# Polysketch attention feeding a gated feed-forward layer: one cast moved to GpSimd, two weight loads moved ahead of a key load, larger dummy products, and a planner's durations rewritten

## The chip, the cores and the metric

The kernel runs on one core of a Trainium2 chip. A core has five engines that run on their own and meet at semaphores: TensorE (PE, with its weight loads shown as PEld), VectorE (DVE), ScalarE (ACT), GpSimd (POOL) and SyncE (SP), which here only issues DMAs. The metric is the device time of one execution in microseconds (us). The profile gives one execution's span, which is a little shorter than its device time.

## The reference

```python
# batch 4, heads 4, seq 1088, head_dim 32, r = 8; x: 4352 tokens x 128; d_ff 1536
def phi(x):                                     # 64 features from 32
    a = np.einsum('rd,bhsd->bhsr', S1, x)
    b = np.einsum('rd,bhsd->bhsr', S2, x)
    return np.einsum('bhsi,bhsj->bhsij', a, b).reshape(*x.shape[:-1], r * r)
q_p, k_p = phi(q), phi(k)
kv  = np.einsum('bhsf,bhsd->bhfd', k_p, v)
num = np.einsum('bhsf,bhfd->bhsd', q_p, kv)
den = np.einsum('bhsf,bhf->bhs', q_p, np.sum(k_p, axis=2))[..., None] + 1e-06
x   = (num / den).transpose(0, 2, 1, 3).reshape(4352, 128)
out = np.maximum(x @ w_gate, 0) * (x @ w_val) @ w_out
```

Inputs and output are float32. The feed-forward part is done with float16 operands, most of the sketches in float32.

## The kernel before, in words

The work has two parts that run through each other. For each of the four batches, attention makes a 128 x 128 block matrix `bz` from keys and values, and then the columns of `xT`, the feed-forward input, from queries. The feed-forward part takes `xT` in groups of two or four blocks of 128 tokens, and each group in units of at most 512 columns.

Keys (class `K`): load `k`, transpose on DVE (L525, `kT`), sketch on PE (`ksk`, L536), transpose back (L549, `kab`), multiply the two sketches out to 64 features (`kphi`, L593, `kp`; POOL for most, DVE for two pieces of batch 0, which first need a copy in PSUM, L557), and sum `kp` times `v` on PE (`kv`, L606). `v` must first be cast to float16 in two halves (`vc`, L599). L613 copies the result to `bz`.

Queries (classes `Q` and `G`): transposes (L1024), sketches (L728), a division by the denominator, then the product to 64 features (`qphi`, L859, `qqp`). The features are transposed (`qpt`), for the first three groups on PE (`qtr`, L877, copied by ACT on L884) and for the other seven by a DMA that SP issues (L867). `num` (L893) multiplies by `bz`, and ACT (L905), or DVE for the first group (L900), writes `xT`. For the first group alone the reciprocals go through ACT (L777), PE (L782) and ACT (L787).

Feed-forward (class `F`), per unit: `g` (L950) and `v` (L962) on PE, relu on ACT (L955), the product `h` on DVE (L972) or, in every sixth unit, a copy on ACT (L967) and the product on POOL (L977), then `o` (L984) on PE. At the end of a group ACT copies the sum (L992) and SP stores it (L1001, L1006).

The weights come as float32, in thirds: `wg0..2`, `wv0..2` (columns) and `wo0..2`. Each third lands in a buffer that later holds the keys, queries or values of batches 1 to 3 (`wst`), and is cast to float16 from there (L425 on ACT, L427 on POOL, by the table `CAST`). So the loads of `v1`, `k2`, `v2`, `k3`, `q3` and `v3` have to wait for casts. All loads, stores and transposing DMAs go through SP's one queue, in program order.

The order of the instructions is not written out by hand. A planner inside the kernel (`Plan`) knows a duration for every step, a landing time for every early load (`LAND`), and a due time for every unit (`T0 + u * U`, plus `D1` from unit 6 on), and lists the steps of each engine in the order in which its own reckoning would start them. Each engine then runs its list strictly in order. The durations change nothing on the chip but this order, and the number of dummy products.

Dummies: `warm(n)` fills the gaps that the planner sees on PE before the first feed-forward unit with products of a zero tile, `n` columns in all, written to a PSUM bank that nothing reads (L330). Their number is fixed when the program is built.

Of the kernel before, what the change touches and what calls it, by code (L numbers as in the profile page):

```python
# [146 lines left out]
def kernel(  # L147
# [115 lines left out]
    load_w(0)  # L263
    load_w(1)
    load_wo(0)
    load_k(nc.sync, 1)
    load_w(2)
    load_wo(1)
    load_wo(2)
    nc.sync.dma_start(out=q_sb[1], in_=flat(q, 1))  # L270
# [55 lines left out]
    def warm(n):  # L326

        while n >= 32:
            m = min(n // 32 * 32, 128)
            nc.tensor.matmul(PS[:, W_BANK, 0:m], zero, zero[:, 0:m], start=True, stop=True)  # L330
            n -= m

    warm(3584)
    S_BANK = 6
# [46 lines left out]
    P.banks[W_BANK] = 13.0  # L381
    P.banks[S_BANK] = 6.0
    l_sx = Lease()
    T0, U, SLACK = 11.0, 0.68, 0.25
    D1 = 0.2

    TURN = ["ACT"] * 3 + ["DMA"] * 7

# [7 lines left out]
        return cols / 960.0 + 0.085  # L396

    def act(cols):
        return cols / 1200.0 + 0.045

    def pool(cols):
        return cols * 0.00188 + 0.07

    LAND = {"k0a": 3.6, "S": 4.3, "k0b": 4.25, "q0a": 5.6, "q0b": 7.35, "v0": 9.95,
            "wg0": 10.35, "wv0": 11.0, "wg1": 11.65, "wv1": 12.3, "wo0": 12.95, "k1": 15.6,
            "wg2": 16.25, "wv2": 16.9, "wo1": 17.5, "wo2": 18.1, "q1": 19.5}
    land = {n: P.landed(n, t) for n, t in LAND.items()}
    P.free["DMA"] = LAND["q1"]

    def bank(l, i=0):  # L410
# [4 lines left out]
    sa_op = P.add("DVE", "SA", 0.22, make_SA, [land["S"]], rec=0.07)  # L415
    wb_op = P.add("DVE", "WB", 0.15, make_WB, [land["S"]], rec=0.07)

    CAST = {"wg0": "ACT", "wv0": "POOL", "wg1": "ACT", "wv1": "POOL", "wo0": "POOL",
            "wg2": "ACT", "wv2": "ACT", "wo1": "ACT", "wo2": "POOL"}
    wcast = {}  # L420

    def cast(w, i, eng):
# [9 lines left out]
                         rec={"ACT": 0.13, "DVE": 0.07, "POOL": 0.0}[e])  # L432


    def load(name, fn, after):
        n = 4 if name[0] == "v" else 1
        i = P.add("SP", f"{name} issue", 0.44 * n, fn, after, rec=1.95 - 0.44 * n)
# [6 lines left out]
    load("k3", lambda: load_k(nc.sync, 3), [wcast["wg0"], wcast["wv0"], land["q2"]])  # L444
    load("q3", lambda: load_q(nc.sync, 3), [wcast["wg1"], wcast["wv1"], land["q2"]])
    load("v3", lambda: load_vs(3), [land["v2"]])

    class K:


        def __init__(self, b, prev):
# [13 lines left out]
                                               [(0, NC // 2), (NC // 2, NC)])]  # L465
            for n, l in enumerate(self.las):
                self.sks.append(P.add(
                    "PE", f"ksk {b} {n}", sk32(KX * 32) + 0.04 if b else (0.62, 0.68)[n],
                    lambda n=n: self.sk(n), t1 + [ws_op], take=[l]))
            if prev is None and b == 0:  # L470
                sx = P.add("PE", "sx", 0.25, make_sx, self.sks, take=[l_sx])
# [13 lines left out]
            self.wc_op = P.add("DVE", f"wc {b}", 0.11, self.wc, [w], drop=[lw], rec=0.07)  # L485
            phis = []
            cut = [(0, 2), (2, 4), (4, 6), (6, KX)] if b else [(0, 2), (2, 4), (4, 6), (6, 8), (8, KX)]
            own = [3, 4] if b == 0 else []
            lb = Lease()
            self.lb = lb  # L490
            for n, (lo, hi) in enumerate(cut):
# [11 lines left out]
                else:  # L503
                    phis.append(P.add("POOL", f"kphi {b} {lo}", pool(cols),
                                      lambda lo=lo, hi=hi: self.phi(nc.gpsimd, lo, hi), dep))
            vc = [P.add("ACT", f"vc {b} {h}", 0.58, lambda h=h: self.vc(h), [land[f"v{b}"]],
                        rec=0.13) for h in range(2)]
            lm = Lease()
            self.lm = lm
            self.kvs = []  # L510
# [87 lines left out]
        def vc(self, h):  # L598
            nc.scalar.copy(out=v16[self.b][:, 2 * h:2 * h + 2], in_=v32[self.b][:, 2 * h:2 * h + 2])  # L599

        def kv(self, lo, hi, pp):
            m = bank(self.lm)
# [28 lines left out]
    class Q:  # L631
# [3 lines left out]
        def __init__(self, b, x0, n, i, ks, qt1, old):  # L635
            self.b, self.x0, self.n, self.ks = b, x0, n, ks
            i = i % NS
            self.abc, self.an = q_abc[i], q_an[i]
            self.dn, self.rd, self.bw = q_dn[i], q_rd[i], bw[i]
            first = b == 0 and x0 == 0  # L640
            self.first = first
            name = f"{b},{x0}"
            cols = n * 32
            wcs = [kk.wc_op for kk in ks]
            if first:
                la, lc = Lease(), Lease()
# [8 lines left out]
                at = P.add("PE", f"qaT {name}", 0.85, self.aT, qt1 + [sa_op], take=[lt])  # L655
                ate = P.add("ACT", f"qaTe {name}", act(256), self.aTe, [at], drop=[lt], rec=0.13)
                s2 = [P.add("PE", f"qc {name}", 0.45, self.cx, [ate, ks[0].zc_op], take=[lc])]
                o1 = P.add("DVE", f"bw {name}", dve(cols) + 0.03, self.mul_ps, s2 + [t2] + old,
                           drop=[lc], rec=0.09)
                e, eng = "DVE", nc.vector  # L660

            else:
                self.l4 = [Lease(2), Lease(2)]
                s1 = P.add("PE", f"qsk {name}", cols / 600.0 + 0.28 + 0.37 * (n > NX),
                           self.sk, qt1 + wcs + [wq_op], take=self.l4)
# [25 lines left out]
            self.t2_op = t2  # L691
            self.last = []
# [106 lines left out]
    class G:  # L799


        def __init__(self, qs, b, ks, x0, n, i, col, old, how):
# [6 lines left out]
            if qs.first:  # L809
                for x in range(n):  # L810
                    phis.append(P.add("DVE", f"qphi {name} {x}", 0.31,
                                      lambda x=x: self.phi(nc.vector, x, x + 1), [qs.o4],
                                      drop=[qs.la], rec=0.07))
                qs.la.left -= n
            else:
                phis.append(P.add("POOL", f"qphi {name}", pool(n * 256),
                                  lambda: self.phi(nc.gpsimd, 0, n), [qs.o4] + old))
            if how == "DMA":
                pt = P.add("SP", f"qtd {name}", 1.28, self.xpose, phis + old, rec=0.7)
                pt = P.add("DMA", f"qtd {name}", 0.6, None, [pt], rec=0.5)  # L820
            else:
                lt = Lease()
# [84 lines left out]
    class F:  # L907


        def __init__(self, u, grp, qg, js, prev, old):  # L910
# [14 lines left out]
            vv = P.add("PE", f"v {u}", cost, self.v, [qg.x_op, wcast[f"wv{third}"]], take=[lv], due=t + 0.2)  # L925
            if self.pool:
                a2 = P.add("ACT", f"vcp {u}", act(cols), self.vcp, [vv], drop=[lv], rec=0.13,
                           due=t + 0.6)
                h = P.add("POOL", f"hp {u}", 1.18, self.hp, [a, a2, old], due=t + 1.3)
# [113 lines left out]
    for n, (b, x0, w, parts) in enumerate(sets):  # L1043
# [6 lines left out]
        for gb, y, m in parts:  # L1050
# [80 lines left out]
```

## Time and profile before

| what | value |
| --- | --- |
| device time, median of 3 runs | 101.46 us (101.31 to 104.93) |
| device time of the profiled execution | 102.56 us |
| its span | 100.8 us |
| PE busy | 95.1 us, 94% of the span |
| DVE, ACT, POOL busy | 83.8, 82.2, 59.9 us |
| bytes moved by DMA | 13.28 MB |
| dummy products (L330) | 85, 7.7 us, all before 14 us |
| granted TensorE clock | 1.00 |

A matmul's printed time holds some 0.2 us that the next one overlaps: one of 512 columns is printed with 0.38 us, and a row of them follows at 0.22 us each. So PE's busy time hides short pauses, which show where one product starts later than the pace of the rows allows. A square bracket in the timeline gives the idle time before an instruction, and who ended it.

### The profile page before, as it was taken

To read this page: it belongs to the slowest core of one execution; us is meant where nothing else is said; L and a number is where in the kernel's file an instruction comes from. 1 tells how busy PE (TensorE), PEld (TensorE's weight loads), DVE (VectorE), ACT (ScalarE), POOL (GpSimd) and SP (SyncE) were. 2 spreads that over 40 slices of the span, in tenths; PEclk is the share of its full clock that TensorE was granted. 3 is DMA by queue.
4 is the path that set the end of the run, shared out by engine and by line. 5 is a ranking of instruction groups with operands and counts; after the bars stand their busy time and mean duration, and the time that the engine had idled before them with its cause. 6 is when DMAs were issued, how large, how long until landed. Compare 5 with 4: busy or idle time off the path is not lost.

```text
span 100.8 us, 3139 instructions
## 1 busy us (share of the span) xinstructions
PE 95.1 (94%) x1191; PEld 66.4 (66%) x1191; DVE 83.8 (83%) x181; ACT 82.2 (82%) x162; POOL 59.9 (59%) x64
## 2 busy tenths in 40 slices
PE   6999997999999899999999999999999999999960
PEld 6959895678775466656756676667666666667940
DVE  5989959899999989999998679978768587795960
ACT  3411968997999978999977769899899999989940
POOL 7157269399999399349973993489960314033100
PEclk9999999999999999999999999999999999999999
DMA  2999999499943696300426003001481300120031
GB/s 44 321 272 294 408 403 417 166 309 272 386 131 108 145 136 163 104 7 0 104 52 156 7 0 104 7 7 37 121 182 37 81 24 0 52 59 0 4 100 52
DMA packets 16783, 13.28 MB, mean 132 GB/s; under 512 B 8064, under 2 KB 14464, under 8 KB 16768
## 3 DMA queue, kind: packets, MB, share of 16 engines
q1 hardware_dynamic: 16736, 13.08, 45.8%
q8 instruction: 9, 0.15, 0.6%
q14 instruction: 6, 0.05, 0.1%
q10 hardware_dynamic: 32, 0.00, 0.0%
HBM read 9.14 MB, written 2.23 MB: 113 GB/s over the span
## 4 chain that ended last, share of the span: by engine, by line
PE 78%; POOL 7%; ACT 5%; DMA 3%; issue 2%; DVE 2%; ACTq 0%
PE ps L984 19%; PE ps L950 18%; PE ps L962 17%; PE ps L330 7%; POOL qqp L859 4%; PE ps L893 3%; ACT g_sb L955 3%; PE ps L728 3%; DMA qpt<-qqp 3%; PE ps L536 2%; PE ps L606 2%; POOL kp L593 1%; PE ps L564 1%; PE ps L877 1%; DVE qabc L734 1%
## 5 line engine op out<-in xcount | busy, mean ns | idle before, releaser
L972 DVE TENSOR_TENSOR ht<-g_sb,ps 128x512 f16<-128x512 f16 (+1 forms) x87 | 55.4, 672 | 10.1 <-ACT g_sb L955 5.5
L955 ACT ACTIVATE g_sb<-ps 128x512 f16<-128x512 f32 (+1 forms) x103 | 57.1, 610 | 4.9 <-PE ps L950 4.1
L950 PE MATMUL ps<-xT,wg 128*128 128x512 f16 (+1 forms) x120 | 38.3, 348 | 0.4 <-ACT wg L425 0.4
L984 PEld LDWEIGHTS <-ht 128*128 128x128 f16 x408 | 28.8, 98 | 14.0 <-POOL ht L977 2.5
L984 PE MATMUL ps<-wo,ht 128*128 128x128 f16 x408 | 36.5, 219 | 0.2
L962 PE MATMUL ps<-xT,wv 128*128 128x512 f16 (+1 forms) x120 | 36.5, 348 | 0.0
L977 POOL TENSOR_TENSOR ht<-g_sb,v_sb 128x512 f16<-128x512 f16 x16 | 18.7, 1170 | 19.3 <-ACT v_sb L967 13.2
L593 POOL TENSOR_TENSOR kp<-kab 128x512 f16<-128x512 f32 (+1 forms) x15 | 17.1, 1162 | 5.0 <-DVE kab L549 5.0
L962 PEld LDWEIGHTS <-wv 128*128 128x128 f16 x120 | 13.0, 115 | 5.1 <-issue 1.1
L859 POOL TENSOR_TENSOR qqp<-qan,qabc 128x1024 f16<-128x1024 f32 (+1 forms) x9 | 15.7, 1763 | 0.1
L950 PEld LDWEIGHTS <-wg 128*128 128x128 f16 x120 | 13.1, 114 | 3.7 <-issue 0.9
L967 ACT COPY v_sb<-ps 128x512 f32<-128x512 f32 x16 | 9.7, 605 | 0.0
L330 PE MATMUL ps<-zero 128*128 128x128 f16 (+2 forms) x85 | 7.7, 257 | 1.0 <-DVE maskkv L295 1.0
L330 PEld LDWEIGHTS <-zero 128*128 128x128 f16 x85 | 6.7, 119 | 1.4 <-DVE maskkv L295 1.0
L992 ACT ACTIVATE o_sb<-ps 128x512 f32<-128x512 f32 (+1 forms) x10 | 5.5, 546 | 1.9 <-PE ps L984 1.9
L599 ACT CAST v<-v 128x576 f16<-128x576 f32 x8 | 5.3, 700 | 1.5 <-DMA v<-in_v_dram 1.4
L734 DVE STREAM_TRANSPOSE qabc<-ps 128x512 f32<-128x512 f32 (+2 forms) x8 | 5.4, 695 | 0.7 <-PE ps L728 0.6
L1024 DVE STREAM_TRANSPOSE qT<-q_sb 128x576 f32<-128x576 f32 (+4 forms) x10 | 6.0, 611 | 0.0
L905 ACT CAST xT<-ps 128x512 f16<-128x512 f32 (+1 forms) x9 | 4.9, 550 | 1.1 <-PE ps L893 1.1
L893 PE MATMUL ps<-qpt,bz 128*128 128x512 f16 (+2 forms) x26 | 5.3, 305 | 0.4 <-DMA qpt<-qqp 0.4
L525 DVE STREAM_TRANSPOSE kT<-k_sb 128x544 f32<-128x544 f32 (+2 forms) x8 | 5.6, 725 | 0.0
L606 PEld LDWEIGHTS <-kp 128*128 128x128 f16 (+1 forms) x72 | 3.6, 98 | 1.3 <-issue 0.2
(85 smaller groups left out, 63.9 us busy)
## 6 DMA issues: line engine op xcount, KB each, us to landing
v<-in_v_dram SPq DMA_DIRECT2D x15, 144.0 KB, 4.5
out_dram<-o_sb SPq DMA_DIRECT2D x28, 64.0 KB, 1.7
k_sb<-in_k_dram SPq DMA_DIRECT2D x3, 544.0 KB, 5.4
q_sb<-in_q_dram SPq DMA_DIRECT2D x3, 544.0 KB, 7.1
k_sb<-in_moe_w_out_dram SPq DMA_DIRECT2D x2, 256.0 KB, 5.9
q_sb<-in_q_dram SPq DMA_DIRECT2D x1, 416.0 KB, 5.2
k_sb<-in_k_dram SPq DMA_DIRECT2D x1, 288.0 KB, 2.9
k_sb<-in_k_dram SPq DMA_DIRECT2D x1, 256.0 KB, 3.0
```

What stands on the lines that cost most here:

```text
L330: nc.tensor.matmul(PS[:, W_BANK, 0:m], zero, zero[:, 0:m], start=True, stop=True)
L593: eng.tensor_tensor(out=self.kp[:, lo:hi].rearrange("p x g (i a c) -> p (x g i) a c", i=2, a=R), in0=src[:, 0, :, :, None].to_broadcast([1 ...
L734: nc.vector.transpose(self.abc[:, 0:self.n, 2 * i:2 * i + 2].rearrange("p x h f -> p h x f"), PS[:, b0:b1 + 1, 0:self.n * 32].rearrange("p ...
L859: eng.tensor_tensor(out=self.qp[:, lo:hi].rearrange("p x g (i a c) -> p (x g i) a c", i=2, a=R), in0=a_in[:, :, :, None].to_broadcast([128 ...
L893: nc.tensor.matmul(o[:, 0:n * 128].rearrange("f (x t) -> f x t", x=n)[:, :, t], self.ks[b or 0].bz[:, p], self.pt[:, 0:n, p, t], start=(p ...
L950: nc.tensor.matmul(bank(self.lg)[:, y * W:(y + 1) * W], wblock(wg, j), x, start=True, stop=True, skip_group_check=True)
L955: nc.scalar.activation(out=self.gs[:, 0:self.cols], in_=bank(self.lg)[:, 0:self.cols], func=ACTF.Relu)
L962: nc.tensor.matmul(bank(self.lv)[:, y * W:(y + 1) * W], wblock(wv, j), x, start=True, stop=True, skip_group_check=True)
L967: nc.scalar.copy(out=self.vs, in_=bank(self.lv))
L972: nc.vector.tensor_tensor(out=self.ht[:, 0:w], in0=self.gs[:, 0:w], in1=bank(self.lv)[:, 0:w], op=ALU.mult)
L977: nc.gpsimd.tensor_tensor(out=self.ht, in0=self.gs, in1=self.vs, op=ALU.mult)
L984: nc.tensor.matmul(o[:, s], self.ht[:, y * W + s * 128:y * W + (s + 1) * 128], wo[:, j // 4, (j % 4) * DM:(j % 4 + 1) * DM], start=(j == 0 ...
```

## The change

- The second half of batch 0's `v` is cast by POOL instead of ACT. In its place POOL casts `wg2`, `wv2` and `wo1`, which ACT did, and ACT casts `wv1`, which POOL did. DVE's share of batch 0's `kphi` goes from two pieces to one; POOL does the other.
- SP issues the loads of `wg2` and `wv2` ahead of batch 1's keys.
- SP issues the loads of `k3`, `q3` and `v3` behind the transposing DMAs of batch 1 (the step `gs[4].turn`), instead of ahead of them.
- A dummy has up to 512 columns, by reading the same 128 columns of zeros up to four times, and before the first unit 0.1 us less is filled in each gap from the time `WARM` on.
- The planner's numbers (`U`, `D1`, `LAND`, `act`, and several steps) are others, so many steps stand elsewhere in their engine's list.

In the built program there are 23 dummies in place of 85, of 8,512 columns in all in place of 10,624. The other products, and the DMAs, are the same in number and size.

```diff
     load_wo(0)
+    load_w(2)
     load_k(nc.sync, 1)
-    load_w(2)
     load_wo(1)
...
         while n >= 32:
-            m = min(n // 32 * 32, 128)
-            nc.tensor.matmul(PS[:, W_BANK, 0:m], zero, zero[:, 0:m], start=True, stop=True)
-            n -= m
+            m, w = (min(n // 128, 4), 128) if n >= 128 else (1, n // 32 * 32)
+            nc.tensor.matmul(PS[:, W_BANK, 0:m * w], zero,
+                             zero[:, None, 0:w].to_broadcast([128, m, w]), start=True, stop=True)
+            n -= m * w
...
-    T0, U, SLACK = 11.0, 0.68, 0.25
-    D1 = 0.2
+    T0, U, SLACK = 11.0, 0.65, 0.25
+    D1 = 0.7
...
-        return cols / 1200.0 + 0.045
+        return cols / 1200.0 + 0.062
...
-            "wg0": 10.35, "wv0": 11.0, "wg1": 11.65, "wv1": 12.3, "wo0": 12.95, "k1": 15.6,
-            "wg2": 16.25, "wv2": 16.9, "wo1": 17.5, "wo2": 18.1, "q1": 19.5}
+            "wv0": 10.99, "wg1": 11.63, "wv1": 12.27, "wo0": 12.91, "wg2": 14.75, "wv2": 15.39,
+            "k1": 16.75, "wo1": 17.39, "wo2": 18.03, "q1": 19.39}
...
-    CAST = {"wg0": "ACT", "wv0": "POOL", "wg1": "ACT", "wv1": "POOL", "wo0": "POOL",
-            "wg2": "ACT", "wv2": "ACT", "wo1": "ACT", "wo2": "POOL"}
+    CAST = {"wg0": "ACT", "wv0": "POOL", "wg1": "ACT", "wv1": "ACT", "wo0": "POOL",
+            "wg2": "POOL", "wv2": "POOL", "wo1": "POOL", "wo2": "POOL"}
...
-            own = [3, 4] if b == 0 else []
+            own = [4] if b == 0 else []
...
-            vc = [P.add("ACT", f"vc {b} {h}", 0.58, lambda h=h: self.vc(h), [land[f"v{b}"]],
-                        rec=0.13) for h in range(2)]
+            vc = [P.add(e, f"vc {b} {h}", 0.66 if e == "POOL" else 0.58,
+                        lambda h=h, e=e: self.vc(h, e), [land[f"v{b}"]],
+                        rec=0.0 if e == "POOL" else 0.13)
+                  for h, e in enumerate(["ACT", "ACT" if b else "POOL"])]
...
+    for n in ("k3", "q3", "v3"):
+        issue[n].after.append(gs[4].turn)
+        gs[4].turn.succ.append(issue[n])
...
-                warm(int((o.start - at) * (1200 if o.start < WARM else 2280)))
+                warm(int((o.start - at) * 1200) if o.start < WARM else
+                     int((o.start - at - 0.1) * 2280))
```

More of the change, by code (lines that the diff above doesn't have):

```diff
@@ L398, in act @@
     def act(cols):
-        return cols / 1200.0 + 0.045
+        return cols / 1200.0 + 0.062
     def pool(cols):
         return cols * 0.00188 + 0.07
-    LAND = {"k0a": 3.6, "S": 4.3, "k0b": 4.25, "q0a": 5.6, "q0b": 7.35, "v0": 9.95,
-            "wg0": 10.35, "wv0": 11.0, "wg1": 11.65, "wv1": 12.3, "wo0": 12.95, "k1": 15.6,
-            "wg2": 16.25, "wv2": 16.9, "wo1": 17.5, "wo2": 18.1, "q1": 19.5}
+    LAND = {"k0a": 3.6, "S": 4.3, "k0b": 4.25, "q0a": 5.4, "q0b": 7.35, "v0": 9.95, "wg0": 10.35,
+            "wv0": 10.99, "wg1": 11.63, "wv1": 12.27, "wo0": 12.91, "wg2": 14.75, "wv2": 15.39,
+            "k1": 16.75, "wo1": 17.39, "wo2": 18.03, "q1": 19.39}
     land = {n: P.landed(n, t) for n, t in LAND.items()}
@@ L432 @@
                          rec={"ACT": 0.13, "DVE": 0.07, "POOL": 0.0}[e])
+    issue = {}
     def load(name, fn, after):
         n = 4 if name[0] == "v" else 1
-        i = P.add("SP", f"{name} issue", 0.44 * n, fn, after, rec=1.95 - 0.44 * n)
+        issue[name] = i = P.add("SP", f"{name} issue", 0.44 * n, fn, after,
+                                rec=1.95 - 0.44 * n)
         land[name] = P.add("DMA", name, 2.7 if n == 4 else 1.4, None, [i], rec=0.15)
@@ L443 @@
     load("v2", lambda: load_vs(2), [wcast["wg2"], wcast["wv2"], land["v1"]])
-    load("k3", lambda: load_k(nc.sync, 3), [wcast["wg0"], wcast["wv0"], land["q2"]])
-    load("q3", lambda: load_q(nc.sync, 3), [wcast["wg1"], wcast["wv1"], land["q2"]])
+    load("k3", lambda: load_k(nc.sync, 3), [wcast["wg0"], wcast["wv0"]])
+    load("q3", lambda: load_q(nc.sync, 3), [wcast["wg1"], wcast["wv1"]])
     load("v3", lambda: load_vs(3), [land["v2"]])
@@ L467, in __init__ @@
                 self.sks.append(P.add(
-                    "PE", f"ksk {b} {n}", sk32(KX * 32) + 0.04 if b else (0.62, 0.68)[n],
+                    "PE", f"ksk {b} {n}", sk32(KX * 32) + 0.04 if b else (0.47, 0.52)[n],
                     lambda n=n: self.sk(n), t1 + [ws_op], take=[l]))
@@ L596, in phi, with vc @@
                 in1=bs[:, :, None, :].to_broadcast([128, n, R, R]), op=ALU.mult)
-        def vc(self, h):
-            nc.scalar.copy(out=v16[self.b][:, 2 * h:2 * h + 2], in_=v32[self.b][:, 2 * h:2 * h + 2])
+        def vc(self, h, e):
+            o, i = (t[self.b][:, 2 * h:2 * h + 2] for t in (v16, v32))
+            nc.scalar.copy(out=o, in_=i) if e == "ACT" else nc.gpsimd.tensor_copy(out=o, in_=i)
         def kv(self, lo, hi, pp):
@@ L654, in __init__ @@
                 self.lt = lt
-                at = P.add("PE", f"qaT {name}", 0.85, self.aT, qt1 + [sa_op], take=[lt])
+                at = P.add("PE", f"qaT {name}", 0.62, self.aT, qt1 + [sa_op], take=[lt])
                 ate = P.add("ACT", f"qaTe {name}", act(256), self.aTe, [at], drop=[lt], rec=0.13)
@@ L663, in __init__ @@
                 self.l4 = [Lease(2), Lease(2)]
-                s1 = P.add("PE", f"qsk {name}", cols / 600.0 + 0.28 + 0.37 * (n > NX),
+                s1 = P.add("PE", f"qsk {name}", cols / 600.0 + 0.34 + 0.37 * (n > NX),
                            self.sk, qt1 + wcs + [wq_op], take=self.l4)
@@ L815, in __init__ @@
             else:
-                phis.append(P.add("POOL", f"qphi {name}", pool(n * 256),
+                phis.append(P.add("POOL", f"qphi {name}", pool(n * 256) - 0.02 * n,
                                   lambda: self.phi(nc.gpsimd, 0, n), [qs.o4] + old))
@@ L819, in __init__ @@
                 pt = P.add("SP", f"qtd {name}", 1.28, self.xpose, phis + old, rec=0.7)
+                self.turn = pt
                 pt = P.add("DMA", f"qtd {name}", 0.6, None, [pt], rec=0.5)
@@ L924, in __init__ @@
                       due=t + 0.35)
-            vv = P.add("PE", f"v {u}", cost, self.v, [qg.x_op, wcast[f"wv{third}"]], take=[lv], due=t + 0.2)
+            vv = P.add("PE", f"v {u}", cost, self.v, [qg.x_op, wcast[f"wv{third}"]], take=[lv], rec=0.07,
+                       due=t + 0.2)
             if self.pool:
@@ L928, in __init__ @@
                            due=t + 0.6)
-                h = P.add("POOL", f"hp {u}", 1.18, self.hp, [a, a2, old], due=t + 1.3)
+                h = P.add("POOL", f"hp {u}", 1.13, self.hp, [a, a2, old], rec=0.06,
+                          due=t + 1.3)
             else:
```

## The prediction

> **What bounds the kernel now.** I read the page first: its busy line, the slices, then the chain.
>
> ```profile
> span 100.8 us, 3139 instructions
> PE 95.1 (94%) x1191; PEld 66.4 (66%) x1191; DVE 83.8 (83%) x181; ACT 82.2 (82%) x162; POOL 59.9 (59%) x64
> PE   6999997999999899999999999999999999999960
> PEclk9999999999999999999999999999999999999999
> PE 78%; POOL 7%; ACT 5%; DMA 3%; issue 2%; DVE 2%; ACTq 0%
> ```
>
> PE sets the time, at a full granted clock, and its useful products are the same before and after. So only three things can move the end: when the first unit starts, where PE pauses after that, and the tail. The slices with less than 9 are at the start, at 15 to 18 us and at the end. The chain in order of time shows the first two (start, us, what):
>
> ```profile
> 12.51 0.22 PE ps L893 x2
> 12.72 1.19 PE ps L330 x22
> 13.91 0.25 PE ps L950 x2
> 14.19 1.58 ACT g_sb L955 x3
> 15.77 0.39 PE ps L877 x4
> 16.19 0.59 ACT qpt L884
> 16.77 0.50 ACT g_sb L955
> 17.27 0.52 ACT wg L425
> 17.83 0.41 PE ps L950 x2
> ...
> 28.17 3.88 POOL qqp L859 x2
> 32.05 0.28 POOL ht L977
> 32.33 2.79 DMA qpt<-qqp
> 35.17 0.60 PE ps L893 x2
> ```
>
> Here dummies (L330) stand between `num` and the first product, and later PE hands over to ACT, to POOL and to a transposing DMA. The timeline says who was late:
>
> ```profile
> 13.40 0.70 POOL L427 CAST wv<-q_sb 128x512 f16<-128x512 f32 x1 [1.82 <-DMA q_sb<-in_moe_w_val_dram]
> 14.62 2.98 POOL L859 TENSOR_TENSOR qqp<-qan,qabc 128x512 f16<-128x512 f32 x2
> 17.16 0.62 ACT L425 CAST wg<-v 128x512 f16<-128x512 f32 x1
> 25.61 4.66 SPq L216 DMA_DIRECT2D v<-in_v_dram  x4
> 30.37 1.79 SPq L1001 DMA_DIRECT2D out_dram<-o_sb  x4
> 32.33 2.68 SPq L867 DMA_TRANSPOSE qpt<-qqp  x2
> ```
>
> POOL waited 1.82 us for `wv1` to land, then cast it and `wo0`, so the second group's features (L859) started at 14.62 though their input (L794, 13.28 + 0.35) was there at 13.63. ACT cast `wg2` only at 17.16. SP was held at the loads of `v2` for 4.66 us and stored a group before it issued the transposes at 32.33; their first input was done at 28.17 + 1.96 = 30.13.
>
> PE's pauses, from start to start less the pace of the rows (256 columns 0.11 us, 128 columns 0.055): between L962 (14.86, two products) and L877 (15.75) 0.67; between L962 (16.43) and L893 (16.82) 0.18; between L984 (17.04, four products) and L950 (17.83) 0.57; between L984 (33.93, twelve) and L893 (35.17) 0.57.
>
> **The change, part by part.**
>
> *Start of the first unit.* Before, `xT` was written by 13.00 + 0.37 = 13.37 (L900), but 22 dummies of 0.056 us ran until 13.79; the first product started at 13.76. After, I follow the chain with the same durations. DVE has one `kphi` piece less (L593, 0.69 printed, 0.60 to the next start), so the reciprocals are ready at about 9.7 instead of 10.27. ACT now expands them (L777) ahead of `v`, not behind two casts of 0.6 each (9.99 to 11.15). POOL has four `kphi` pieces from 6.45 at 1.03 each, to 10.6, then half of `v`. The trace has no such cast on POOL: the nearest row is L427, 0.61 for 512 columns, so 576 take 0.69; the upper bound is the rate of POOL's two-input rows, 1.07 for 512, so 1.2. I take 0.69, as this is a cast too: `v` is ready at 11.3. Then 18 `kv` products at 0.029 (to 11.8), L613 (0.30), `num` (12.16, 0.4 with its latency), L900 (0.37): `xT` at about 13.0. The dummies left there are 1,440 columns, 0.6 us from 12.4, and end at 13.0 as well. So the first product comes at about 13.05: **0.7 sooner**. The upper bound of `v` costs 0.5 of it.
>
> *A wait that this brings.* `wv1` is cast by ACT now, in order, ahead of the first relu. SP issues the loads up to `wo0` as before, so it lands at about 13.4 again, whatever `LAND` says (12.27). ACT is then done at 13.9, and the first relu starts at 13.9, against 14.19. Behind it wait three relus and the copy on L884, and PE, which has six banks to fill before it needs ACT. So part of the 0.7 comes back as pauses of PE at 14.4 to 16.
>
> *Pauses until 18 us.* POOL no longer waits for `wv1`: it casts `wv0` to 11.9 and starts L859 when L794 is done, at 13.25, 1.4 sooner. It casts `wo0`, `wg2` and `wv2` from 14.3, at 0.58 from start to start, so `wg2` is ready at 15.5, if it has landed: it takes the place in the queue that `k1` had, behind `wo0` (cast at 14.05), so about 14.6. So the pauses of 0.67 and 0.57, both POOL's or ACT's lateness with a cast, go. What is late next is ACT itself: four copies of 0.48 from 13.9 leave PE short by some 0.4 before 15.4, and by 0.2 to 0.3 twice more until 18. Together 0.9 against 1.42: **0.5 gained**.
>
> *`k1` behind two weight thirds.* Two thirds are 512 KB, 1.3 us at the 400 GB/s of the slices there. `kT` (L525) started at 16.02 and will start by 17.3. It is covered: what waits for `kab` is POOL's `kphi` (21.05 before), and POOL is busy until 20.3 now. Without that cover the delay of up to 1.3 would go on to the transposes of batch 1.
>
> *POOL's load, 10 to 30 us.* Added: one `kphi` (1.03), half of `v` (0.65), `wg2`, `wv2`, `wo1` (3 x 0.58); removed: `wv1` (0.58): 2.8 us. POOL idled 1.43 + 1.82 + 0.21 + 1.50 = 5.0 us there by its brackets, so it fits, but `h` on POOL (L977) comes later beside it, and so do `wo1` and `wo2`, on which the loads of `k2` and `v1` wait (`v1` issued at 20.3, not 19.33). PE waited for POOL's `h` 8 times for 2.5 us, 0.5 at the longest: I charge one more such wait, **0.35 lost**, between 0 and 0.7.
>
> *The transposes.* `k3`, `q3` and `v3` go behind them, so the loads of `v2` no longer wait for the 1.1 MB of `k3` and `q3`, and SP is through with the second store at about 30.0 (its copy at 28.2, plus 1.8). L859 for batch 1 is done near 29.7. So the transposes start 2 us sooner and land by 33, before PE asks. That takes away the 0.57 at 34.5, and up to 0.4 of the short waits for ACT and DVE at 39 to 43: **0.6 gained**, between 0.4 and 1.0. `k3` is now issued at about 34 and lands, with the 5.4 to 7.1 us of its rows, by 41; `kT` for batch 3 was last made at 46.5. `v3` was cast until 44.1 and has later places in ACT's list now. If these were late, ACT would hold relus behind `v3`; there are 3 us of room.
>
> *Dummies.* The first 28, at 0.113 each (3.17), become seven of 512 columns at the same rate, 3.0 us; the start is bound by the keys' transposes (L525, until 5.0), so at most 0.15 is gained, and I count 0. *The rest of the order* (36 to 94 us) has the same products with PE already dense: 0, within 0.3 either way. At the end the last products on DVE stand one place otherwise: 0.15 lost.
>
> Row against rule: L794 on DVE, with two inputs in SBUF, ran from 13.28 beside POOL's cast of 13.40, and that cast took 0.70 where others took 0.61. [...]
>
> **Sum.** 0.7 + 0.5 - 0.35 + 0.6 - 0.15 = 1.3 us. The profiled execution took 102.56, of which the span is 100.8 and 1.8 lies around it; the sum makes it 101.3, with a span of 99.5. The median of the runs is 1.1 below the profiled execution. I carry the 1.3 over unchanged: 101.46 - 1.3 = 100.2.
>
> **The rivals.**
>
> *A: more comes through.* The short waits that followed the late transposes go too (1.0 instead of 0.6), POOL's lateness costs nothing (0 instead of 0.35), and the store and load traffic is thinner. 1.3 + 0.4 + 0.35 = 2.05: 99.4. For it: SP's 4.66 us was the longest hold in its queue. Against: ACT and POOL are nearly full from 14 to 30 us in the new order.
>
> *B: hidden.* ACT's wait for `wv1` decides, not the start: the relus gain only 14.19 - 13.9 = 0.3, and the transposes 0.4, less 0.15: 0.5, so 100.9. For it: the chain has ACT right behind the first product. Against: both pauses at 15 to 18 had another cause than the first relu.
>
> *C: POOL becomes the bound, and it is slower.* From 13.3 to 30 us POOL's list has almost no gaps left. What it loses there passes to `qqp` of batch 1 and the transposes, and PE runs out of units. With casts at the 0.70 of the one disturbed row, seven cost 0.6 and eat half of the sum. PE asked for the first of these at 34.6 before, and would ask some 0.85 sooner, at 33.75, so landing at 33 leaves 0.7 of cover: the gain is gone when POOL is 0.7 + 1.3 = 2.0 us later by 30 us than I reckon. With six casts of weights at the two-input rate (0.46 more each) and `v` 0.5 more, POOL is 3.3 later and the time 101.46 + 1.3 = 102.8. For it: POOL took 0.09 more beside DVE once. Against: its other casts hold 0.61 to a hundredth.
>
> *D: it doesn't do what it says.* If `k3` and `q3` weren't what held SP, the transposes stay at 32; that is B or worse and is counted there.
>
> **How the numbers follow.** Forecast 0.48 (its own range 99.7 to 100.7), A 0.2, B 0.22, C 0.1. The range, 98.9 to 101.9, takes in A and B with their bounds and the near half of C. A measurement of this kernel can tell about 2% from no change, here 99.4 and 103.5: faster by more 0.23 (A and the lower edge of the forecast), slower by more 0.05, within 0.72.
>
> **What would show it.** Right: first L950 near 13.1; the first L955 near 13.9, with ACT idle before it for `wv1`'s DMA; L859 near 13.3; no PE wait for `wg2`; the first L867 near 30 and no pause before L893 of batch 1. Wrong: POOL's casts above 0.65; L867 still past 31; pauses of PE above 0.5 between 18 and 34; a lower granted clock; ACT waiting for `v3`.

## The result, and the profile after

| | before | after |
| --- | --- | --- |
| median of 20 runs | 102.23 us (101.31 to 104.93) | 101.21 us (100.56 to 101.65) |
| profiled execution, its span | 102.56, 100.8 | 101.53, 99.8 |

The ratio of the times is 0.992 (0.989 to 0.995): the change makes the kernel 0.8% faster, 1.0 us in the medians and 1.0 us in the profiled executions. The forecast was 1.3 us, to 100.2 us. Of the 1.0 us by which the time lies above that, 0.77 is the starting point: 101.46 was the median of three runs, and with 20 runs it is 102.23. The rest is the sum's. Medians here are of all runs, while the ratios, with their 95% intervals, leave out runs that took over 1.5% more than the fastest of their kernel, so the two need not agree. Line numbers from the first changed line on are 1 to 10 higher than before (cast of `v` L606, transposing DMA L875, `num` L901, `g` L960, `v` L972, store L1011); the other versions' numbers lie within a few of these or of those before.

The page of the changed kernel, its first lines and the chain's shares:

```profile
span 99.8 us, 3035 instructions
PE 94.0 (94%) x1129; PEld 61.6 (62%) x1129; DVE 83.5 (84%) x180; ACT 81.3 (82%) x159; POOL 62.6 (63%) x68
...
PE 79%; DVE 6%; ACT 5%; DMA 3%; SPq 3%; issue 2%; ACTq 0%
```

PE is still what bounds the kernel. New in the chain is SP's queue with 3%, where POOL had 7%. The chain in order of time (start, us, what) shows where:

```profile
13.03 0.35 PE ps L960 x2
...
28.23 1.42 SPq L1011
...
30.77 2.82 DMA qpt<-qqp
...
33.63 0.60 PE ps L901 x2
```

The first `g` stands behind `num` and dummies as before, 0.76 us sooner (13.00 by the timeline). Then comes a passage that the chain of before had with POOL: a store on SP, the transposing DMA behind it, and `num` of batch 1. The timeline (start, us, engine and line, idle time before in brackets):

```profile
10.94 0.62 POOL L428 CAST wv<-k_sb 128x512 f16<-128x512 f32 x1
11.02 0.75 DVE L769 TENSOR_TENSOR bw<-qabc 128x192 f32<-128x192 f32 x1
12.17 0.62 ACT L426 CAST wv<-q_sb 128x512 f16<-128x512 f32 x1
13.29 1.07 POOL L867 TENSOR_TENSOR qqp<-qan,qabc 128x512 f16<-128x512 f32 x1 [1.74 <-DVE qan L801]
13.42 1.57 ACT L965 ACTIVATE g_sb<-ps 128x512 f16<-128x512 f32 x3 [0.62 <-PE ps L960]
14.86 0.61 POOL L428 CAST wg<-v 128x512 f16<-128x512 f32 x1
27.86 2.73 SPq L1011 DMA_DIRECT2D out_dram<-o_sb  x4
30.77 3.00 SPq L875 DMA_TRANSPOSE qpt<-qqp  x2
93.52 3.45 SPq L1011 DMA_DIRECT2D out_dram<-o_sb  x4
97.06 0.38 SPq L1016 DMA_DIRECT2D out_dram<-o_sb  x1
```

POOL no longer waits for `wv1` to land, and `wg2` is cast at 14.86, not 17.16. ACT's first relu waits for PE, not for `wv1`. The transposes are issued at 30.77, where 32.33 was before. Four stores that took 1.79 us to issue took 2.73 here, and 3.45 at the end.

What PE gained, by where it stood in its work, was 0.76 us at the first product, 1.36 when 35% of the columns of `g` were done (44.49, before 45.86), 1.42 at 80% and 1.40 at the start of the last product (96.08, before 97.48). The two lists take these columns in different orders (at half of them the difference is only 0.20), so the fractions are rough. But PE's pauses of 0.05 us and more after 45 us add up to 2.60, before 2.61, so the gain is made before then and kept. Of it 0.37 is lost behind the last product: 3.68 us remain there, 3.31 before.

### The profile page after: what moved, and what is told of

Same layout as the page of the kernel before. It is cut to its first block, busy times and chain, and to the rows that moved or that the text cites. A ratio compares the mean times of both kernels' runs of the same rounds, so it can differ in the third digit from the quotient of the medians.

```text
span 99.8 us, 3035 instructions
## 1 busy us (share of the span) xinstructions
PE 94.0 (94%) x1129; PEld 61.6 (62%) x1129; DVE 83.5 (84%) x180; ACT 81.3 (82%) x159; POOL 62.6 (63%) x68
## 4 chain that ended last, share of the span: by engine, by line
PE 79%; DVE 6%; ACT 5%; DMA 3%; SPq 3%; issue 2%; ACTq 0%
PE ps L994 21%; PE ps L960 21%; PE ps L972 19%; PE ps L330 5%; PE ps L901 4%; DMA qpt<-qqp 3%; SPq L1011 3%; PE ps L735 2%; ACT g_sb L965 2%; PE ps L542 2%; ACT v L606 1%; PE ps L613 1%; DVE qabc L741 1%; PE ps L885 1%; DVE qT L1034 1%
## 5 line engine op out<-in xcount | busy, mean ns | idle before, releaser
L960 PE MATMUL ps<-xT,wg 128*128 128x512 f16 (+1 forms) x120 | 38.9, 348 | 0.1
L972 PE MATMUL ps<-xT,wv 128*128 128x512 f16 (+1 forms) x120 | 38.7, 347 | 0.0
L599 POOL TENSOR_TENSOR kp<-kab 128x512 f16<-128x512 f32 (+1 forms) x16 | 18.0, 1154 | 2.5 <-DVE kab L555 2.5
L867 POOL TENSOR_TENSOR qqp<-qan,qabc 128x1024 f16<-128x1024 f32 (+1 forms) x9 | 15.8, 1760 | 2.0 <-DVE qan L801 1.7
L972 PEld LDWEIGHTS <-wv 128*128 128x128 f16 x120 | 13.4, 114 | 3.2 <-issue 0.4
L960 PEld LDWEIGHTS <-wg 128*128 128x128 f16 x120 | 13.3, 114 | 3.2 <-issue 1.1
L330 PE MATMUL ps<-zero 128*128 128x512 f16 (+5 forms) x23 | 6.7, 417 | 1.0 <-DVE maskkv L295 1.0
L901 PE MATMUL ps<-qpt,bz 128*128 128x512 f16 (+2 forms) x26 | 5.3, 306 | 0.9 <-DMA qpt<-qqp 0.8
L606 ACT CAST v<-v 128x576 f16<-128x576 f32 x7 | 4.6, 690 | 0.0
L330 PEld LDWEIGHTS <-zero 128*128 128x128 f16 x23 | 2.3, 117 | 3.0 <-issue 1.4
L613 PE MATMUL ps<-v,kp 128*128 128x64 f16 (+1 forms) x72 | 4.2, 192 | 0.0
```

What stands on the lines that cost most here:

```text
L330: nc.tensor.matmul(PS[:, W_BANK, 0:m * w], zero, zero[:, None, 0:w].to_broadcast([128, m, w]), start=True, stop=True)
L599: eng.tensor_tensor(out=self.kp[:, lo:hi].rearrange("p x g (i a c) -> p (x g i) a c", i=2, a=R), in0=src[:, 0, :, :, None].to_broadcast([1 ...
L867: eng.tensor_tensor(out=self.qp[:, lo:hi].rearrange("p x g (i a c) -> p (x g i) a c", i=2, a=R), in0=a_in[:, :, :, None].to_broadcast([128 ...
L901: nc.tensor.matmul(o[:, 0:n * 128].rearrange("f (x t) -> f x t", x=n)[:, :, t], self.ks[b or 0].bz[:, p], self.pt[:, 0:n, p, t], start=(p ...
L960: nc.tensor.matmul(bank(self.lg)[:, y * W:(y + 1) * W], wblock(wg, j), x, start=True, stop=True, skip_group_check=True)
L972: nc.tensor.matmul(bank(self.lv)[:, y * W:(y + 1) * W], wblock(wv, j), x, start=True, stop=True, skip_group_check=True)
```

## The experiments

The first theory, S, says that SP's queue decides when batch 1's transposes start, and with them how much of the early gain comes through. The second, F, came from the trace's DMA records: besides the data there are packets of 16,384 bytes on an "instruction" queue (q8), nine in this profile, the first at 12.76 us. From the first to the ninth PE starts 1,935 weight loads and products, 242 for each packet. That mean is 238 to 249 in every profile of this case, however many dummies it has, so the packets fit PE's program being fetched as it runs. They are called code packets below. F says that these packets disturb the DMAs beside them, so that the number of PE's instructions, and with it the dummies, moves a disturbance through the kernel. All ratios are to the kernel before on the same chip; "against after" is a ratio divided by 0.992, and with the intervals of both taken as independent it is uncertain by 0.5 to 0.8 points either way.

**Small dummies in the changed kernel.**

```diff
-            m, w = (min(n // 128, 4), 128) if n >= 128 else (1, n // 32 * 32)
...
+            m = min(n // 32 * 32, 128)
+            nc.tensor.matmul(PS[:, W_BANK, 0:m], zero, zero[:, 0:m], start=True, stop=True)
```

> The changed kernel with its dummies in pieces of 128 columns again; every other instruction stands in the same order. Theory F (a fetch of PE's program, one 16 KB packet of about 1 us on one of the 16 DMA engines, holds up the loads queued behind it, and 60 fewer dummies moved it from 10.8 to 12.8 us): the q8 packet is back near 10.8 us or earlier, wv1 lands near 13.3 and not 11.7, ACT casts it near 13.3 and not 12.17, the first relu starts near 13.9 and not 13.42, and the time is 0.2 to 0.5 us above the changed kernel. Rival V (the landing of wv1 varies by chance from execution to execution): the landing has nothing to do with the dummies, wv1 is cast at 12.2 in this profile as in the changed kernel's, and the time is the same within 0.1 us.

Measured: 100.74 us, ratio 0.990 (0.984 to 0.995), which cannot be told from the changed kernel's; one of the six runs took 514.98 us, and why is not known. So the times show no gain from the larger dummies by themselves. The first packet was back, at 9.98, but `wv1` was cast at 12.73 without a wait, so the expectation of a late `wv1` failed. Another packet had moved as well: the one that fell at 27.95 in the changed kernel came at 24.72. SP's timeline and the chain (start, us, what):

```profile
28.16 1.75 SPq L1010 DMA_DIRECT2D out_dram<-o_sb  x4
30.08 3.98 SPq L874 DMA_TRANSPOSE qpt<-qqp  x2
```

```profile
32.91 0.22 PE ps L993 x4
33.14 0.43 PE ps L900 x2
```

The four stores took 1.75 us to issue, not 2.73, the transposes started at 30.08, and PE went from `o` to `num` of batch 1 without a pause, at 32.98 by the timeline, although its first product had come 0.29 later than in the changed kernel. Only 3.29 us remained behind the last product. The order on SP is that of the changed kernel, so it is the store held beside a packet that made the pause before `num` in that kernel's profile.

**Large dummies in the kernel before.** The same three lines, the other way round.

> The kernel before with nothing changed but the dummies, up to 512 columns each. Theory F: the q8 packet near 10.8 us comes 1.5 to 2.5 us later, wv1 lands at 11.7 to 12.0, POOL casts it by 12.1 and not 13.40, the features of the second group start near 13.65 and not 14.62, the pause of 0.67 before PE's transposes at 15.75 shrinks below 0.2, and the time falls by 0.3 to 0.7 us. Rival V: no change beyond 0.1 us, and wv1 lands where chance puts it.

Measured: 104.14 us, ratio 1.012 (1.005 to 1.020): slower, from an edit that takes 59 products away. The early part went the way theory F had it, if later: `wv1` landed at 12.49, was cast at 12.55, and the pause of 0.67 is gone. But the profiled execution, with 104.71 one of six between 102.40 and 106.59, lost more later. SP's timeline and PE's longest wait in the stretch where 2.2 us were lost:

```profile
69.37 2.98 SPq L1002 DMA_DIRECT2D out_dram<-o_sb  x3
72.88 1.27 SPq L868 DMA_TRANSPOSE qpt<-qqp  x1
```

```profile
PE ps L894 <- DMA qpt<-qqp: 2.1, 1, 2.1
```

One store of the three, at 69.85, took 2.03 us to issue, beside a code packet of 1.62 us at 69.88. The transposing DMA behind it went out at 72.88 instead of 71.39 and took 3.25 us to land, and PE stood still for 2.2 us. The features had been ready. Whether the other five executions lost their time at the same place is not shown.

**Large dummies, but as many PE instructions as before.** Each product of 512 columns becomes one of 416 and three of 32.

```diff
+            v = w - 32 * (m - 1) // m // 8 * 8
+            nc.tensor.matmul(PS[:, W_BANK, 0:m * v], zero, ...)
+            for _ in range(m - 1):
+                nc.tensor.matmul(PS[:, W_BANK, 0:32], zero, zero[:, 0:32], start=True, stop=True)
```

> The kernel before with dummies of up to 512 columns, but each wide dummy followed by small ones of 32 columns, so that PE's list has exactly as many instructions as before. Theory F (PE's code comes in 16 KB packets, one for so many instructions, and a DMA that SP issues beside such a packet takes 1.1 to 2.1 us to issue instead of 0.43): the packets are back within 0.3 us of where the kernel before has them (10.8, 16.8, 26.6, 34.7, 44.5, 56.4, 63.7, 76.5), no store is held at 69.9, the transposes for the num at 74 are issued at 71.4, and the time is that of the kernel before, 102.0 within 0.4. Rival W (the wide dummies themselves cost the time, whatever the packets do): 104.1, as with wide dummies alone.

Measured: 102.45 us beside 102.45, ratio 1.001 (0.996 to 1.006). With the number of instructions restored the loss is gone, though the dummies stay wide. That speaks for F and against W. Its profiled execution had a granted clock of 0.67 and took 137.64 us, so times in it cannot be compared, but places in PE's list can. Counted in the weight loads and products that PE still has to start, the last eight packets come 4 to 34 sooner than in the kernel before (the first 85 sooner); with wide dummies alone they come 68 to 178 later.

**`k3`, `q3`, `v3` ahead of the transposes again**, in the changed kernel; `k3` and `q3` wait for the landing of `q2` again, as they did before:

```diff
-    for n in ("k3", "q3", "v3"):
-        issue[n].after.append(gs[4].turn)
-        gs[4].turn.succ.append(issue[n])
```

> The changed kernel with k3, q3 and v3 free of the transposes again, as before; k3 and q3 then stand ahead of v2 in SP's queue. Theory S (SP's queue decides when the first transposes of batch 1 are issued): the first transpose is issued at 32 us or later instead of 30.77, PE's pause before num of batch 1 grows from 0.96 to 2 us or more, and the time rises by 0.6 to 1.2 us. Rival P (POOL's features decide, and SP's move bought nothing): the transpose stays near 30.8, the time within 0.2 us.

Measured: 104.17 us, ratio 1.012 (1.005 to 1.020), 2.1% against after. The direction is S's, the mechanism is another: the first transposing DMA was issued at 30.94, hardly later than 30.77. The waits from 30 to 40 us (us in total, times, longest; L606 is the cast of `v`):

```profile
ACT v L606 <- DMA v<-in_v_dram: 3.1, 1, 3.1
...
PE ps L972 <- ACT g_sb L965: 2.7, 1, 2.7
```

The last part of `v2` was issued behind `k3` and `q3`, at 26.47, where the changed kernel had it at 25.32, and landed later still. Of its 16 pieces 15 were there at 32.36 and the last at 33.39, beside a code packet at 31.14; in the changed kernel all were there at 28.57. ACT, whose list has the cast of `v2` ahead of the next relus, stood for 3.1 us, and PE for want of banks behind it. Then came what the windows show (start and end, length, busy us of PE, PEld, DVE, ACT, POOL with instructions, granted clock, DMA share, GB/s):

```profile
33.00:34.00 1.00, 0.00 (x0) 0.00 (x0) 0.00 (x0) 0.51 (x1) 0.00 (x0) 1.00 0.65 136
...
35.00:36.00 1.00, 1.00 (x4) 0.35 (x3) 1.00 (x3) 0.90 (x3) 0.00 (x0) 0.50 0.98 278
```

After the pause PE ran at half its clock until about 37.9. That execution took 105.40; the other five, of which there is no trace, took 102.49 to 105.21. How the loss divides between the pause and the clock is not shown.

**The second group's stores behind the first transposing DMA**, in the changed kernel; only SP's order changes.

```diff
+    late = [f for f in fs if f.last][1].st_op
+    late.after.append(gs[3].turn)
+    gs[3].turn.succ.append(late)
```

> The changed kernel with one more order on SP: the second group's four stores go behind the first transposing DMA of batch 1; nothing else moves on any engine. In the changed kernel these stores took SP from 27.86 to 30.59, and the features were ready at 29.46. Theory S: the transpose is issued near 29.5 and lands near 32.3, the pause of 0.96 before num of batch 1 falls below 0.2, and the time falls by 0.5 to 0.9 us. Rival P: ACT or POOL is late next, the pause stays as pauses of 0.2 to 0.3 around it, and the time falls by less than 0.3 us.

Measured: 100.17 us, ratio 0.985 (0.979 to 0.990). SP's timeline and the chain there:

```profile
29.32 1.32 SPq L875 DMA_TRANSPOSE qpt<-qqp  x1
30.75 1.93 SPq L1011 DMA_DIRECT2D out_dram<-o_sb  x4
```

```profile
32.44 0.22 PE ps L994 x4
32.67 0.43 PE ps L901 x2
```

The DMA now goes out when its features are done, and PE goes from `o` to `num` without a pause. The last product began at 94.97, 1.10 us ahead of the changed kernel; 0.96 of that is the pause that is gone, and 0.16 a first product that came sooner. This shows S for the changed kernel: with the stores behind, a held store no longer holds the transposing DMA. Against after it is 0.7% faster (0.1 to 1.3%), and with the next version it is the fastest tried.

**Both: stores behind, and small dummies.**

> The changed kernel with the second group's stores behind the first transposing DMA, and with dummies of 128 columns. Theory S and F together: the first transposing DMA is issued at 29.4, num of batch 1 starts at 32.2 to 32.5, and the last code packet falls near 89.5, off the last stores, so that the span ends 2.7 to 3.2 us after the last product instead of 3.7: 99.7. Rival: the two do not add, since with 128 columns the packet at 24.7 holds the load of v2 and the last store was held for another reason: 100.2 to 100.7.

Measured: 100.70 us beside 102.45, ratio 0.985 (0.981 to 0.990). The first transposing DMA went out at 29.39 and the last packet fell at 89.95, off the last stores, as expected; `num` came at 32.56, and 3.30 us remained behind the last product, not 2.7 to 3.2. It is no faster than the last version: that one, too, kept only 3.34 us there, with a packet at 93.86. The two do not add.

**The casts undone**, in the changed kernel:

```diff
-            own = [4] if b == 0 else []
+            own = [3, 4] if b == 0 else []
...
-                  for h, e in enumerate(["ACT", "ACT" if b else "POOL"])]
+                  for h, e in enumerate(["ACT", "ACT"])]
```

and the table `CAST` of before.

> The changed kernel with the casts where they were: both halves of v and wg2, wv2, wo1 on ACT, wv1 on POOL, two pieces of kphi on DVE; loads, turn and durations stay changed. Theory T (what the start gains passes to the end in full): the first product at 13.7 instead of 13.0, pauses of PE until 18 us of 1.0 to 1.4 instead of 0.6, and 1.0 to 1.4 us more in the time: 102.2 to 102.6. Rival H (hidden: the transposes of batch 1 set when PE goes on, whatever the start): num of batch 1 at 33.6 as in the changed kernel and the time within 0.3 of it, 100.7 to 101.3.

Measured: 103.18 us, ratio 1.011 (1.004 to 1.018), 2.0% against after: more than either theory had. The first product came at 13.55, 0.55 later. The waits from 16 to 28 us show the larger part:

```profile
ACT v L606 <- DMA v<-in_v_dram: 1.8, 1, 1.8
...
PE ps L960 <- ACT g_sb L965: 1.3, 1, 1.3
```

Here it is `v1` for which ACT stood (L606), in a list that the planner made with other casts in it.

**`wv0` cast by ACT too**, so that POOL is idle beside `bw` (L769): `"wv0": "ACT"` in the table.

> The changed kernel with wv0 cast by ACT too, so that POOL runs nothing between its half of v and the second group's features while DVE multiplies bw (L769). Lock (the two hold each other up): L769 takes 0.35 us instead of 0.47 to 0.75, and xT is there 0.1 to 0.4 us sooner; the time falls by as much if it passes through (100.8), or stays at 101.0 to 101.2 if the dummies ahead of the first product or ACT's fourth cast (0.52 more, the first relu at 13.6 to 13.9) use it up. Rival (no lock: L769 was long for another reason): L769 stays at 0.7 and the first product at 13.0.

Measured: 102.02 us, ratio 1.001 (0.997 to 1.005), 1.0% against after. DVE's line there:

```profile
11.46 0.34 DVE L769 TENSOR_TENSOR bw<-qabc 128x192 f32<-128x192 f32 x1
```

0.34 with POOL idle, 0.75 beside POOL's cast. The other traces agree. In the kernel before (L762 there) the product began at 11.98, when POOL's cast (10.97, 0.61) was over, and took 0.35. Where a cast on POOL was already running, the same product took 0.66 to 0.75 in six versions, and 0.47 in one where only the last 0.26 us of the cast fell beside it. Where it began 0.24 to 0.25 us ahead of the cast (large dummies in the kernel before, casts undone), it took 0.35, and the cast its usual 0.61 to 0.62. So the product took longer only where the cast had begun first; a cast that took as much longer beside it is seen nowhere. That execution was 0.44 late with the queries' transposes already (8.08, not 7.64), and the first product came only 0.17 late (13.17), so some 0.3 us did pass to the start. The time went up all the same: behind four casts ACT's third relu came at 15.50 instead of 14.39, and PE paused 0.92 at 16.9. What the longer product alone costs in the end was not isolated; getting rid of it this way costs more.

**The order of the loads undone**, `load_w(2)` behind `load_k(nc.sync, 1)` and the landing times with it:

> The changed kernel with the loads of wg2 and wv2 behind batch 1's keys again (and the planner's landing times for these three put back with them). Theory L (the order of the loads is worth something because POOL's cast of wg2 is what the second group waits for): wg2 lands near 16, POOL casts it at 16 to 16.3 instead of 14.9 and holds wv2, wo1 and the features behind it; PE pauses 0.5 to 1.0 more before 18 us, and the time is 101.5 to 102.0 beside 101.0 for the changed kernel on this chip. Rival (hidden: PE has other units until then): within 0.2 of the changed kernel.

Measured: 101.99 us beside 102.51, ratio 0.998 (0.995 to 1.002), 0.7% against after, as theory L had it in size. `wg2` was cast at 17.79. It stands in POOL's list behind 1.96 us of features, as the planner was told of a later landing. That profiled execution was 1.0 us late from 7 us on, before any of the moved loads, so its times are not compared further, and what costs the 0.7% is not shown.

**The turn alone, in the kernel before.** The lines of the turn added, for `k3`, `q3` and `v3`, in place of the wait of `k3` and `q3` for the landing of `q2`; nothing else.

> The kernel before with one part of the change alone: k3 and q3 are issued behind the transposing DMAs of batch 1. Theory S (SP's queue held them): the first transposing DMA is issued at 30.0 to 30.3 instead of 32.3, the pause of 0.57 at 34.5 goes, and the time falls by 0.4 to 0.7, to 101.5. Rival N (a part alone does not pay, because the lists of all engines are made for the whole): the transposes come sooner, but num moves with them or k3 comes late, and the time is that of the kernel before, 102.0 to 102.6, or worse.

Measured: 102.55 us beside 102.51, ratio 1.001 (0.997 to 1.004): nothing, rival N. The profiled execution, the fastest of its twelve with 101.68, had the first transposing DMA at 30.87 and `num` at 33.95 instead of 35.17, without a pause before it; over all runs no gain is left.

**The planner's durations of before, in the changed kernel.**

```diff
-    T0, U, SLACK = 11.0, 0.65, 0.25
-    D1 = 0.7
+    T0, U, SLACK = 11.0, 0.68, 0.25
+    D1 = 0.2
```

and with them the durations of `act`, the key sketches, `qaT`, `qsk`, `qphi`, `v` and `hp`.

> The changed kernel with the planner's durations, U and D1 of the kernel before; casts, loads, turn and dummies stay changed. Theory P (the lists fit the chip only with the durations as profiled): PE asks for results before they are there, pauses above 0.5 us appear between 14 and 45 us, and the time is 102.0 or more. Rival (the parts that move work make the gain; durations are worth little): the time is within 0.3 of the changed kernel, 100.8 to 101.3.

Measured: 104.28 us, ratio 1.018 (1.011 to 1.025), 2.7% against after. Two pauses stand out in the profile: 1.2 us near 25, where ACT waited 1.7 us for `v1` to land, and 1.1 us at 74, behind transposes issued at 72.66, after a store that took 1.80 us beside a packet at 70.33.

## Why the prediction was right or wrong

All terms below are of the two profiled executions, 102.56 and 101.53 us, each 0.3 above its kernel's median. Pauses are counted as in the prediction, from 0.05 us on. Of six profiles whose start is made of the same work (the changed kernel's among them), five have the first product between 12.84 and 13.29 and one at 14.03, so a tenth of a microsecond in a term means little.

*Start, forecast 0.7: right, in part by luck.* It is 0.76, and as reckoned the dummies end (13.0) when `xT` is there (12.94). On the way two errors cancelled: `v` was ready 0.3 sooner than I took it, and L769 lasted 0.4 longer than the row of before (0.75; L762, 0.35). In the traces this product took 0.34 to 0.35 alone, and 0.66 to 0.75 where a cast on POOL was already running. So the longer product was no loss against the forecast, since `v` was sooner by about as much.

*ACT's wait for `wv1`: wrong.* I had the first relu at 13.9, because `wv1` landed at 13.35 before. It came at 13.42: `wv1` landed at 11.74, and ACT cast it at 12.17 without waiting. The traces suggest what had made it late. The load comes in 16 pieces. Before, 15 of them were there 4.84 us after the issue and the last after 6.02, beside the code packet at 10.79. In four of the 13 profiles the last piece came 0.81 to 1.36 us behind the one before it, and each of the four had a packet at 10.1 to 10.8, with the load in flight. In the other nine it came 0.03 to 0.15 behind, and the whole load took 4.41 to 4.97 us; two of these had a packet in flight too, so each late piece had an overlap, but not each overlap a late piece. With 23 dummies in place of 85 PE reached its first packet at 12.76, after `wv1` had landed. So the late landing that the prediction carried over went with the place of that packet, and the place with the number of PE's instructions, which the change lowers. Rival B falls as well: where `wv1` was late in a changed kernel (stores behind, small dummies) ACT waited 0.65 us for it, and the first relu still came 0.45 behind the first product, against 0.42.

*Pauses until 18 us, forecast 0.5: right in mechanism, too small.* They are 0.62 us in all, before 1.51 (the prediction's 1.42 has only the three largest): 0.89 gained. L867 at 13.29 (13.25 reckoned) and `wg2` at 14.86 are as followed; the surplus fits the wait for `wv1` that did not come.

*POOL's load, forecast -0.35:* about -0.09, the pauses from 18 to 30 us (1.75, before 1.66). POOL kept up (its casts of weights took 0.61 to 0.62 each), and batch 1's features were done at 29.46, 29.7 reckoned. Rival C is out. The delays that the prediction called covered were so: `kT` of batch 1 started at 16.61 (17.3 reckoned), and `k3` was issued at 33.81 and landed at 38.1 (41 reckoned).

*The transposes, forecast 0.6: the step that failed.* The pauses from 30 to 45 us are 2.42, before 2.31: -0.11. The prediction had SP through with the second store at 30.0, its copy plus 1.8 us, and the transposes landed by 33, before PE asks. The copy was done 0.4 sooner than reckoned, but the stores took 2.73 us to issue, since one of the four took 1.42 beside the packet at 27.95. So the first transposing DMA left at 30.77, 1.3 us after its features were done, and landed at 33.6. And PE asked at 32.67, not at 33.75: start, pauses and load had given some 1.6 us, not 0.85, and the rest of the 1.9 us by which it asked sooner (34.6 before) is the new list, which has `num` earlier. So the pause in front of `num` did not go, it grew from 0.57 to 0.96, and the shorter pauses around it gave only 0.28 back. Two versions show that the held store is the cause. With small dummies no packet fell on the stores, and with the stores behind they no longer stood in the way; in both the pause is gone, and the pauses from 30 to 45 us are 1.46 and 1.45, some 0.85 below before, within the 0.4 to 1.0 that the step had promised.

*Rest and tail, forecast -0.15:* PE's last part gave +0.01, but the end lost 0.37, which the sum did not have: the last four stores took 3.45 us to issue instead of 1.77, one of them 2.12 beside a packet at 95.06, and the final store went out 0.98 us behind the last product, not 0.66. Holds of up to 1.8 us at the same place cost nothing in other versions (3.30 to 3.34 us behind the last product).

0.76 + 0.89 - 0.09 - 0.11 + 0.01 = 1.46, of which 1.40 is there at the last product: 0.06 is not assigned to a term. 1.40 - 0.37 = 1.03, the gain of the two profiled executions. The held stores, before `num` and at the end, are seen in this one execution; its 20 runs went from 100.56 to 101.65, and whether the faster ones had them is not shown.

What the sum could not show is that its terms are not parts that can be had singly. Taken back one at a time, the casts cost 2.0%, the turn 2.1%, the order of the loads 0.7% and the durations 2.7%, where all together gained 0.8%; the turn alone, in the kernel before, gained nothing. Three of these losses have one form in the profile: ACT stands at the cast of a `v` that has not landed, with relus behind it in its list. That lists which fit the times on the chip are worth something is shown by the durations, which change nothing there but the lists and a few dummy columns (8,704, not 8,512). That the casts and the turn lose by their lists, and not by the moved parts themselves, is only suggested: the planner makes new lists with every such edit, and no run kept the lists.

## What to carry to other kernels

The time that a queue needs to issue a DMA is no constant: here the four stores of a group took 1.75 to 3.45 us. When a wait is taken away, look up what is next in the same queue, with its own length, and compare it with the time at which the bound engine will ask after all the other gains, not after the gain of this step alone. In a kernel whose engines run fixed lists, price a part together with the lists made for it. Put a DMA on which the bound engine waits ahead of stores that nobody waits for: that one swap on SP was worth 0.7% (0.1 to 1.3%), beside 0.8% for the whole change.

## What the runs showed of the hardware

The packets on the instruction queue fit PE's program arriving while it runs: 16,384 bytes each, one for 238 to 249 weight loads and products in the mean of a profile. Some DMAs beside them took longer. The view of DMA queues of the changed kernel, for 27.9 to 29.4 us (packets, MB, share of 16 engines):

```profile
q8 instruction: 1, 0.02, 5.5%
```

| kernel | packet: start, us | issue on SP beside it: start, us |
| --- | --- | --- |
| before | 26.60, 1.06 | `v2`, 26.61, 1.43 |
| after | 27.95, 1.31 | store, 28.23, 1.42 |
| after | 95.06, 1.54 | store, 94.85, 2.12 |
| small dummies | 24.72, 1.11 | `v2`, 24.66, 1.56 |
| large dummies in before | 69.88, 1.62 | store, 69.85, 2.03 |

In twelve profiles (all but the one at a clock of 0.67) SP issued 694 loads and stores after 9 us. 44 took over 0.8 us to issue, and each of the 44 overlapped such a packet; of those that overlapped none the longest took 0.74, and the median 0.43. 48 more overlapped one and were not held, so each hold had an overlap, but not each overlap a hold; what decides was not tried. PE stood still for 2.2 us once behind a store held in this way (large dummies in before). Some loads in flight were late too: beside a packet the last of a load's 16 pieces came up to 1.36 us behind the others (`wv1`, above).

PE's granted clock fell to 0.50 at the end of a pause of 2.7 us and stayed there for some 3 us (34.45 to 37.86, `k3` ahead again); after the pause of 2.2 us (large dummies) it stayed at 1.00.
